# Linear attention on one core: v in whole rows, a touch of sixteen pieces, and a tenth warm-up matmul

## The chip, the cores and the metric

The kernel runs on one core of a Trainium2 chip. Its time is the device time of that core in microseconds (us), and the time of a kernel is the median of its runs. The engines named below are TensorE (PE for its matmuls, PEld for its weight loads), VectorE (DVE), ScalarE (ACT), GpSimd (POOL) and SyncE (SP), which here only issues transfers. Sixteen DMA engines move the data.

## What is computed

Inputs q, k and v have the shape (1, 32, 2048, 128) in bf16: 32 heads of 2048 rows by 128 columns. Each head is computed alone.

```python
phi_q = jnp.where(q > 0, q + 1, jnp.exp(q)) + 1e-6
phi_k = jnp.where(k > 0, k + 1, jnp.exp(k)) + 1e-6
kv = jnp.einsum("bhsd,bhse->bhde", phi_k, v)
z = jnp.einsum("bhsd->bhd", phi_k)
num = jnp.einsum("bhqd,bhde->bhqe", phi_q, kv)
den = jnp.einsum("bhqd,bhd->bhq", phi_q, z)[..., None] + 1e-6
return num / den
```

## The kernel before

Every engine gets a list of operations, each with a key; a small planner (`Plan`) sorts each engine's list by key and puts in the semaphore waits that the reads and writes ask for. TensorE's part of heads 1 to 30 is a hardware loop of five turns of six heads.

A head is cut into 16 tiles of 128 rows: partition p holds rows 16p to 16p+15, so that one partition's share of a head is 4 KB that lie together in memory. The feature map is split in two parts that are never added in full: `emk` = min(exp(k), 1) + 1e-6 and `rk` = max(k, 0), and the same for q with `emq` and `rq`. Per head the steps are these.

- SP issues the loads of k, q and v (line 386, 512 KB each) into six buffers each, `h % 6`. The first in its queue are k0, q0, v0, k1, q1, v1.
- ACT: `ek` = exp(k) (line 393). DVE: `emk` from it (line 399). POOL: `rk` (line 396; head 1 on DVE), and for tiles 1 to 5 (`ADD`) the sum of both parts (line 404).
- TensorE transposes the 16 tiles of q into `xT_ps` (line 432, "tr(h)"). ACT makes `eq` = exp of that (line 443; in head 0 in two halves), ACT and DVE make `rq` (lines 450, 452), DVE `emq` (line 464).
- TensorE multiplies phi_k by v into `kvz_ps` (line 414, "kv(h)"), for the 11 tiles of `SPLIT` once with `emk` and once with `rk`, for the five of `ADD` once with the sum. ACT copies the 128 columns to `kvs_sb` (line 423), DVE the z column (line 425, key "zs").
- TensorE multiplies phi_q by `kvs_sb` into `o_ps` ("num(h)", lines 480 and 481), and DVE divides (lines 502 to 524). SP stores the head (line 566).

In TensorE's list the order is tr(0), kv(0), tr(1), kv(1), num(0), tr(2), kv(2), num(1) and so on.

The sum z needs a column of ones beside v. In a v buffer, gaps of 32 columns that hold ones lie between groups of tiles: with GROUPS[buffer] = 1 there is a gap ahead of tile 0 and one behind tile 15; with 2 there is another between tiles 7 and 8. A tile at the edge of a group gets z from a matmul of 129 columns in place of 128, one gap column included. Every other tile needs one more matmul with the same weights, of a single column of ones (`mm_held`, line 344). With two groups v is loaded in half rows of 2 KB (lines 383 to 386). GROUPS is (1, 1, 1, 1, 2, 2), so heads with `h % 6` of 4 or 5 have half rows.

Ahead of the first head, TensorE runs nine matmuls of 500 columns on zeros ("warm-ups", lines 354 to 361; all but the first are at line 344). ACT's first instruction is a transfer of 64 bytes of v into a small tile of its own, `first_sb` (line 372, "the touch"); kv(0) has this transfer among the things it waits for.

Of the kernel before, what the change touches and what calls it, by code (L numbers as in the profile page):

```python
# [12 lines left out]
def _ap(base: bass.AP, elem_offset: int, dims):  # L13
    return bass.AP(base.tensor, base.offset + elem_offset, [list(base.ap[0])] + [list(d) for d in dims])
# [235 lines left out]
def bass_standalone__linear_attn_elu__prompt_kernel(  # L250
# [6 lines left out]
    B, H, S, D = q.shape  # L257
    assert D == P and S == 16 * P
    NT = 16
    NH = B * H  # L260
    bf16 = mybir.dt.bfloat16
    fp32 = mybir.dt.float32
    NBI = 6
# [7 lines left out]
    ADD = (1, 2, 3, 4, 5)  # L271
    SPLIT = tuple(j for j in range(NT) if j not in ADD)
    GAP = 32
    GROUPS = (1, 1, 1, 1, 2, 2)
    VW = NT * D + 3 * GAP

    qf = q.rearrange("b h s d -> (b h) s d")
    kf = k.rearrange("b h s d -> (b h) s d")
    vf = v.rearrange("b h s d -> (b h) s d")
    of = out.rearrange("b h s d -> (b h) s d")  # L280

    with ExitStack() as es:  # L282
        def sb(name, shape, dt):
            return es.enter_context(nc.sbuf_tensor(name, shape, dt))

        k_sb = sb("k_sb", [P, NBI, NT * D], bf16)
        v_sb = sb("v_sb", [P, NBI, VW], bf16)
        q_sb = sb("q_sb", [P, NBI, NT * D], bf16)
# [9 lines left out]
        o_sb = sb("o_sb", [P, NBO, NT, D], bf16)  # L298
        ident = sb("ident", [P, P], bf16)
        ones_sb = sb("ones_sb", [P, 1], bf16)  # L300
        first_sb = sb("first_sb", [1, 64], bf16)

        xT_ps = es.enter_context(nc.psum_tensor("xT_ps", [P, NT * P], bf16))
        kvz_ps = es.enter_context(nc.psum_tensor("kvz_ps", [P, 512], fp32))
# [14 lines left out]
        pl = Plan()  # L319
# [4 lines left out]
        vfull, ofull = v_sb[:, :, :], o_ps[:, :]  # L324
        xfull = xT_ps[:, :].bitcast(fp32)

        def vcol(bi, j):
            n = NT // GROUPS[bi]
            return GAP * (j // n + 1) + D * j, j % n == 0, j % n == n - 1
# [8 lines left out]
               reads=[("id0",)], writes=[("ident",)])  # L338
        n1 = GROUPS.count(1)
        pl.add("pool", -7, lambda g: g.memset(_ap(vfull, 0, [[VW, n1], [GAP + NT * D, 2], [1, GAP]]), 1.0), writes=[("vones", 1)])  # L340
        pl.add("pool", -6.5, lambda g: g.memset(_ap(vfull, n1 * VW, [[VW, NBI - n1], [GAP + NT * D // 2, 3], [1, GAP]]), 1.0),
               writes=[("vones", 2)])
        def mm_held(pe, out_ap, rhs, stop, start=False):
            return pe.add_instruction(mybir.InstMatmult(  # L344
                start_tensor_calc=start, stop_tensor_calc=stop, ldweights=False, bass_skip_group_check=True,
                tile_position=(0, 0), tile_size=(P, P), name=nc.get_next_instruction_name(), engine=mybir.EngineType.PE,
                ins=[pe.lower_ap(rhs), pe.lower_ap(held[0])], outs=[pe.lower_ap(out_ap)]))

        held = [None]
        WARM = 9  # L350

        def warm(pe):
            held[0] = zero_sb
            zeros = _ap(zero_sb, 0, [[0, 4], [1, 125]])
            for w in range(WARM):
                b = 2 + w % 3
# [12 lines left out]
                 ("zs", LAST): LAST - 1 + 0.902, ("kvs", LAST): LAST - 1 + 0.72}  # L369
        halves = {}  # L370

        pl.add("act", -20, lambda a: a.dma_start(first_sb[:, 32:64], vf[0, 0:1, 0:32]), writes=[("first",)], dma=("va", 0))

        for h in range(NH):
            def at(name, key, h=h):
                return place.get((name, h), h + key)
# [3 lines left out]
            def load(name, buf, src, key, h=h, bi=bi):  # L380
                dst, rws = buf[:, bi], rows(src, h)
                if name == "v":
                    n = GROUPS[bi]
                    dst = _ap(vfull, bi * VW + GAP, [[GAP + NT * D // n, n], [1, NT * D // n]])
                    rws = rws.rearrange("p (a b) -> p a b", a=n)
# [22 lines left out]
            def kv(pe, tiles, srcs, bi=bi, b3=b3):  # L408
                for j in tiles:
                    for src in srcs:  # L410
                        first, fin = (j == SPLIT[0] and src is emk_sb), j == ADD[-1]
                        w = src[:, b3, j * D:(j + 1) * D]
                        c, l, r = vcol(bi, j)
                        last = pe.matmul(kvz_ps[:, 1 - l:NC + r], lhsT=w, rhs=v_sb[:, bi, c - l:c + D + r], start=first, stop=fin,  # L414
                                         skip_group_check=True)
                        if not l + r:
                            held[0] = w
                            last = mm_held(pe, kvz_ps[:, 0:1], ones_sb[:, 0:1], fin)
                return last
            pl.add("pe", at("kv", -1.2), lambda pe, kv=kv: kv(pe, SPLIT, (emk_sb, rk_sb)),  # L420
                   reads=[("emk", b3), ("rk", b3), ("v", bi), ("ones",), ("vones", GROUPS[bi])] + ([("first",)] if h == 0 else []), writes=[("bankkv",)])
            pl.add("pe", at("kv", -1.2), lambda pe, kv=kv: kv(pe, ADD, (rk_sb,)), reads=[("phik", b3), ("v", bi)], writes=[("bankkv",)])
# [183 lines left out]
```

## Time and profile before

| | |
|---|---|
| median of 3 runs | 169.97 us (169.88 to 170.01) |
| the profiled execution | 169.75 us |
| its span in the profile | 168.0 us |
| PE busy | 159.1 us, 95% of the span |
| PEld / DVE / ACT / POOL busy | 91% / 90% / 93% / 62% |
| DMA queue 1 (all loads and stores) | 67.12 MB in 19856 packets, 99.0% of 16 engines |
| DMA queue 10 (the touch) | 2 packets |
| mean rate over the span | 400 GB/s |

Busy shares are averages over the start, the steady state and the end. A matmul's recorded duration is its latency, 217 ns for 128 columns, while matmuls that follow one another start 56 ns apart; so the pace is read from starts. "Idle before" names what ended the wait that came just ahead of an instruction.

### The profile page before, as it was taken

Reading aid. Unit: us, or ns where it says so; the run is one execution under the profiler, and the core shown is the slowest. Engines: PE = TensorE matmul, PEld = TensorE weight load, DVE = VectorE, ACT = ScalarE, POOL = GpSimd, SP = SyncE. Lnnn points to the kernel's source line nnn. Section 1 sums busy time; section 2 is a strip of 40 time slices with the busy share of each in tenths; the row PEclk is TensorE's granted clock in tenths of the full one; section 3 lists DMA queues with packets and bytes.
Section 4 is the critical chain, followed back from the end, with each engine's and each line's share of the span. In section 5 each row is a group of like instructions: output and inputs, shape, how many; then the busy total and the mean of one; then the engine's idle time right before and its main releaser. Section 6 shows DMA issues by size and latency. Waiting matters only on the chain.

```text
span 168.0 us, 6551 instructions
## 1 busy us (share of the span) xinstructions
PE 159.1 (95%) x3169; PEld 153.3 (91%) x2465; DVE 151.9 (90%) x298; ACT 155.6 (93%) x143; POOL 103.5 (62%) x71
## 2 busy tenths in 40 slices
PE   7689999999999999999999999999999999999960
PEld 0479999999999999999999999999999999999950
DVE  0367999999999999999999999999999999999971
ACT  3879999999999999999999999999999999997790
POOL 2717677666666777666667766666677766666300
PEclk9999999999999999999999999999999999999995
DMA  5999999999999999999999999999999999999955
GB/s 201 355 419 417 418 407 420 414 411 416 419 415 420 421 415 419 419 418 417 419 418 419 419 415 419 418 417 419 419 419 419 419 418 418 419 419 416 414 244 197
DMA packets 19869, 67.25 MB, mean 400 GB/s; under 512 B 2066, under 2 KB 2194, under 8 KB 19858
## 3 DMA queue, kind: packets, MB, share of 16 engines
q1 hardware_dynamic: 19856, 67.12, 99.0%
q8 instruction: 5, 0.08, 0.2%
q14 instruction: 6, 0.05, 0.1%
q10 hardware_dynamic: 2, 0.00, 0.0%
HBM read 50.33 MB, written 16.78 MB: 400 GB/s over the span
## 4 chain that ended last, share of the span: by engine, by line
PE 89%; DMA 4%; DVE 2%; ACT 1%; SPq 1%; issue 0%; DVEq 0%
PE kvz_ps L414 37%; PE o_ps L480 18%; PE o_ps L481 17%; PE xT_ps L432 16%; DMA k_sb<-in_k_dram 4%; DVE o_sb L520 1%; PE kvz_ps L344 1%; ACT ek_sb L393 1%; SPq L386 1%; DVE emk_sb L399 0%; DVE rden_sb L508 0%; DVE den_sb L502 0%; DVE o_sb L513 0%; DVEq L282 0%; DVE kvs_sb L425 0%
## 5 line engine op out<-in xcount | busy, mean ns | idle before, releaser
L404 POOL TENSOR_TENSOR rk_sb<-rk_sb,emk_sb 128x640 bf16<-128x640 bf16 x32 | 44.7, 1396 | 50.2 <-DVE emq_sb L464 44.5
L414 PE MATMUL kvz_ps<-v_sb,rk_sb 128*128 128x128 bf16 (+1 forms) x512 | 69.1, 217 | 0.0
L520 DVE TENSOR_TENSOR o_sb<-o_ps,rden_sb 128x768 bf16<-128x768 f32 (+2 forms) x62 | 67.8, 1134 | 0.0
L393 ACT ACTIVATE ek_sb<-k_sb 128x2048 bf16<-128x2048 bf16 x32 | 61.5, 1920 | 2.5 <-DMA k_sb<-in_k_dram 2.4
L443 ACT ACTIVATE eq_sb<-xT_ps 128x2048 bf16<-128x2048 bf16 (+1 forms) x33 | 60.1, 1825 | 3.7 <-PE xT_ps L432 2.5
L480 PE MATMUL o_ps<-kvs_sb,emq_sb 128*128 128x129 bf16 (+1 forms) x536 | 61.1, 217 | 0.2 <-DVE o_sb L513 0.2
L481 PE MATMUL o_ps<-kvs_sb,rq_sb 128*128 128x129 bf16 (+1 forms) x536 | 61.1, 217 | 0.0
L396 POOL TENSOR_SCALAR rk_sb<-k_sb 128x2048 bf16<-128x2048 bf16 x31 | 58.7, 1893 | 2.3 <-DMA k_sb<-in_k_dram 2.3
L344 PE MATMUL kvz_ps<-ones_sb,rk_sb 128*128 128x1 bf16 x428 | 59.6, 165 | 0.0
L414 PE MATMUL kvz_ps<-v_sb,emk_sb 128*128 128x128 bf16 (+1 forms) x352 | 56.8, 218 | 1.6 <-DMA v_sb<-in_v_dram 1.1
L480 PEld LDWEIGHTS o_ps<-kvs_sb,emq_sb 128*128 128x128 bf16 x536 | 50.6, 98 | 0.5 <-DVE o_sb L513 0.4
L481 PEld LDWEIGHTS o_ps<-kvs_sb,rq_sb 128*128 128x128 bf16 x536 | 50.1, 97 | 0.0
L414 PEld LDWEIGHTS kvz_ps<-v_sb,rk_sb 128*128 128x128 bf16 x512 | 46.7, 96 | 1.1
L344 PE MATMUL kvz_ps<-ones_sb,emk_sb 128*128 128x1 bf16 x268 | 44.0, 165 | 0.0
L414 PEld LDWEIGHTS kvz_ps<-v_sb,emk_sb 128*128 128x128 bf16 x352 | 33.8, 96 | 1.9 <-issue 1.2
L432 PE MATMUL xT_ps<-ident,q_sb 128*128 128x128 bf16 x512 | 34.5, 222 | 0.4 <-DMA q_sb<-in_q_dram 0.4
L432 PEld LDWEIGHTS xT_ps<-ident,q_sb 128*128 128x128 bf16 x512 | 30.6, 99 | 4.4 <-DMA q_sb<-in_q_dram 4.4
L450 ACT ACTIVATE rq_sb<-xT_ps 128x1024 bf16<-128x1024 bf16 x30 | 30.6, 1019 | 0.0
L399 DVE TENSOR_SCALAR emk_sb<-ek_sb 128x2048 bf16<-128x2048 bf16 x32 | 21.9, 684 | 6.0 <-ACT ek_sb L393 6.0
L452 DVE TENSOR_SCALAR rq_sb<-xT_ps 128x1024 bf16<-128x1024 bf16 x34 | 23.4, 691 | 2.8 <-ACT eq_sb L443 2.4
L464 DVE TENSOR_SCALAR emq_sb<-eq_sb 128x2048 bf16<-128x2048 bf16 x32 | 22.4, 699 | 0.0
L513 DVE TENSOR_TENSOR o_sb<-o_ps,rden_sb 128x128 bf16<-128x128 f32 x31 | 9.0, 291 | 1.1
(28 smaller groups left out, 47.6 us busy)
## 6 DMA issues: line engine op xcount, KB each, us to landing
k_sb<-in_k_dram SPq DMA_DIRECT2D x32, 512.0 KB, 14.3
q_sb<-in_q_dram SPq DMA_DIRECT2D x32, 512.0 KB, 14.1
v_sb<-in_v_dram SPq DMA_DIRECT2D x32, 512.0 KB, 14.3
out_dram<-o_sb SPq DMA_DIRECT2D x31, 512.0 KB, 14.9
out_dram<-o_sb SPq DMA_DIRECT2D x1, 288.0 KB, 3.3
out_dram<-o_sb SPq DMA_DIRECT2D x1, 224.0 KB, 3.2
first_sb<-in_v_dram ACTq DMA_DIRECT2D x1, 0.1 KB
```

What stands on the lines that cost most here:

```text
L344: return pe.add_instruction(mybir.InstMatmult(start_tensor_calc=start, stop_tensor_calc=stop, ldweights=False, bass_skip_group_check=True, ...
L393: lambda a, bi=bi, b2=b2: a.activation(ek_sb[:, b2, :], k_sb[:, bi, :], ACT.Exp),
L396: lambda e, bi=bi, b3=b3: e.tensor_scalar(rk_sb[:, b3, :], k_sb[:, bi, :], BIG, 0.0, op0=ALU.min, op1=ALU.max),
L404: pl.add("pool", h + 0.5, lambda g, added=added: g.tensor_tensor(out=added(rk_sb), in0=added(rk_sb), in1=added(emk_sb), op=ALU.add), reads ...
L414: last = pe.matmul(kvz_ps[:, 1 - l:NC + r], lhsT=w, rhs=v_sb[:, bi, c - l:c + D + r], start=first, stop=fin, skip_group_check=True)
L432: last = pe.transpose(xT_ps[:, j * P:(j + 1) * P], q_sb[:, bi, j * P:(j + 1) * P], ident[:])
L443: halves[part] = pl.add("act", key, lambda a: a.activation(eq_sb[:, b2, c], xT_ps[:, c], ACT.Exp), reads=both[part:part + 1] or both, writ ...
L450: f = lambda a: a.activation(rq_sb[:, b3, c], xT_ps[:, c], ACT.Relu)
L452: f = lambda d: d.tensor_scalar(rq_sb[:, b3, c], xT_ps[:, c], 0.0, None, op0=ALU.max)
L480: pe.matmul(o_ap, lhsT=emq_sb[:, b3, t * P:(t + 1) * P], rhs=kvs_sb[:, b3, c0:c1], start=True, stop=False)
L481: return pe.matmul(o_ap, lhsT=rq_sb[:, b3, t * P:(t + 1) * P], rhs=kvs_sb[:, b3, c0:c1], start=False, stop=True)
L520: pl.add("dve", key, lambda d: d.tensor_tensor(out=o_sb[:, bo, 3 * g0:3 * g1, :].rearrange("p (a b) d -> p a b d", b=3), in0=_ap(full, bas ...
```

## The change

All six v buffers have one group, so every v is loaded in whole rows of 4 KB, and the gaps of ones are two in each buffer. One POOL memset fills them; the second memset is gone. The touch reads 32 columns from each of 16 places of head 0's v, 32 KB apart, into 16 partitions. The warm-up has ten matmuls.

```diff
-    GROUPS = (1, 1, 1, 1, 2, 2)
-    VW = NT * D + 3 * GAP
+    GROUPS = (1, 1, 1, 1, 1, 1)
+    VW = NT * D + 2 * GAP
...
-        first_sb = sb("first_sb", [1, 64], bf16)
+        first_sb = sb("first_sb", [16, 64], bf16)
...
         pl.add("pool", -7, lambda g: g.memset(_ap(vfull, 0, [[VW, n1], [GAP + NT * D, 2], [1, GAP]]), 1.0), writes=[("vones", 1)])
-        pl.add("pool", -6.5, lambda g: g.memset(_ap(vfull, n1 * VW, [[VW, NBI - n1], [GAP + NT * D // 2, 3], [1, GAP]]), 1.0),
-               writes=[("vones", 2)])
...
-        WARM = 9
+        WARM = 10
...
-        pl.add("act", -20, lambda a: a.dma_start(first_sb[:, 32:64], vf[0, 0:1, 0:32]), writes=[("first",)], dma=("va", 0))
+        pl.add("act", -20, lambda a: a.dma_start(first_sb[:, 32:64], vf[0].rearrange("(p j) d -> p (j d)", p=NT)[:, 0:32]), writes=[("first",)], dma=("va", 0))
```

The order of the instructions on every engine stays as it was, apart from the memset that is gone, the added warm-up and four more single-column matmuls in each head of buffers 4 and 5.

## The prediction

> **What bounds the kernel now.** The chain of waits comes first: 89% of the span is TensorE work.
>
> ```profile
> PE 89%; DMA 4%; DVE 2%; ACT 1%; SPq 1%; issue 0%; DVEq 0%
> ```
>
> The list of waits from 12.1 to 160 us comes next. TensorE (PE, and PEld for its weight loads) waits only once there, for 0.5 us at 12.0 us; it never waits for a transfer.
>
> ```profile
> POOL rk_sb L404 <- DVE emq_sb L464: 44.5, 29, 1.8
> ...
> PEld kvz_ps L414 <- DVE kvs_sb L425: 0.7, 1, 0.7
> PE kvz_ps L414 <- DVE kvs_sb L425: 0.5, 1, 0.5
> ```
>
> So two things set the end: when kv(1), the KV product of head 1, starts (12.03), and how much TensorE work follows. For the second I cut the steady state into heads, from one head's first transpose to the next, and asked for the instructions on kvz_ps alone. Each row holds the stretch, its length, then busy time and count on PE, PEld, DVE and ACT. Head 8's transposes start at 44.91, and the rows below are heads 8 to 12.
>
> ```profile
> 44.91:49.75 4.84, 2.25 (x50) 2.12 (x27) 0.22 (x1) 0.29 (x1) 1.00 1.04 418
> 49.75:54.57 4.82, 2.25 (x50) 2.12 (x27) 0.22 (x1) 0.29 (x1) 1.00 1.04 419
> 54.57:59.30 4.73, 2.15 (x46) 2.01 (x27) 0.22 (x1) 0.29 (x1) 1.00 1.02 418
> 59.30:64.04 4.74, 2.15 (x46) 2.01 (x27) 0.21 (x1) 0.29 (x1) 1.00 1.02 416
> 64.04:68.86 4.82, 2.25 (x50) 2.12 (x27) 0.22 (x1) 0.29 (x1) 1.00 1.03 419
> ```
>
> The third and fourth rows are heads 10 and 11, whose v lies in buffers 4 and 5, in half rows: four matmuls fewer on kvz_ps, 0.10 us less PE time on it, and a head that is 0.08 to 0.11 us shorter. TensorE is busy through all of every stretch, so it is the bound in both kinds of head.
>
> For the start I read the timeline from 0 to 16 us (start, duration, engine, instruction, idle time before it in brackets).
>
> ```profile
> 4.12 1.91 ACT L393 ACTIVATE ek_sb<-k_sb 128x2048 bf16<-128x2048 bf16 x1 [1.56 <-DMA k_sb<-in_k_dram]
> 5.33 1.75 PE L432 MATMUL xT_ps<-ident,q_sb 128*128 128x128 bf16 x16 [0.38 <-DMA q_sb<-in_q_dram]
> 6.41 1.94 ACT L443 ACTIVATE eq_sb<-xT_ps 128x1024 bf16<-128x1024 bf16 x2 [0.38 <-PE xT_ps L432]
> 8.19 0.22 PE L414 MATMUL kvz_ps<-v_sb,emk_sb 128*128 128x129 bf16 x1 [1.10 <-DMA v_sb<-in_v_dram]
> 9.20 1.91 ACT L393 ACTIVATE ek_sb<-k_sb 128x2048 bf16<-128x2048 bf16 x1 [0.85 <-DMA k_sb<-in_k_dram]
> 11.14 0.69 DVE L399 TENSOR_SCALAR emk_sb<-ek_sb 128x2048 bf16<-128x2048 bf16 x1 [0.87 <-ACT ek_sb L393]
> 11.75 0.22 DVE L425 TENSOR_SCALAR kvs_sb<-kvz_ps 128x1 bf16<-128x1 f32 x1
> ```
>
> Head 1's k lands, ACT's exp of it runs from 9.20, DVE makes emk(1) from 11.14, then the z column of head 0, and only then kv(1) starts at 12.03. ACT stood idle 0.85 us before 9.20, after eq(0) ended at 8.35.
>
> Why is k late? The transfers are queued k0, q0, v0, k1, q1. Their times to landing, each asked for alone, are 3.4, 4.1, 6.3, 7.1 and 7.8 us; with the issue times 0.73, 1.18, 1.65, 2.11 and 2.59 they land at about 4.1, 5.3, 7.95, 9.2 and 10.4. All steps are 1.2 us but one: v0 comes 2.65 us behind q0, 1.4 too many, and all behind it are late by as much. In the trace's completion marks of the sixteen DMA engines, twelve had finished v0 by 6.77 and four came at 7.32, 7.45, 7.91 and 7.94. The DMA view of 5 to 8 us beside that of 8 to 11 says the same.
>
> ```profile
> DMA packets 281, 1.04 MB, mean 345 GB/s; under 512 B 28, under 2 KB 28, under 8 KB 281
> ...
> DMA packets 340, 1.25 MB, mean 418 GB/s; under 512 B 34, under 2 KB 34, under 8 KB 340
> ```
>
> The engines were busy 99% or more in both: packets took longer, nothing was missing in the queue.
>
> **Part 1, whole rows.** Ten of the 32 heads use buffers 4 and 5 (4, 5, 10, 11, 16, 17, 22, 23, 28, 29). In each, tiles 7 and 8 stop being edges: four 129-column matmuls become 128 wide, and four 128x1 matmuls are added, 50 in place of 46. From the starts of the transposes, 17 whole-row heads from 6 to 30 take 4.826 us on average and the eight half-row ones 4.735: +0.091 each. By single starts, a 128-column matmul with its 128x1 companion takes 0.082 and one alone 0.056, so 4 x 0.026 = +0.105 less four columns. I take the head period, since it holds everything: 10 x 0.091 = **+0.91 us**, bounds 0.85 and 1.05. Nothing covers it, as TensorE never waits there; ACT and DVE, busy 4.74 and 4.73 of head 9's 4.82 us, stay below. The DMA side, ten transfers in 128 pieces fewer each, shortens a queue for which TensorE doesn't wait, so 0; and it has an idle stretch of its own at 162 to 163 us (53 GB/s) ahead of the last stores. The POOL memset that goes (0.26 us at 1.65) and the one that grows lie inside POOL's 2.27 us of waiting for k0: 0.
>
> **Part 2, the touch.** Before, it moves one piece (queue 10 has 2 packets: data and semaphore), so one DMA engine meets v ahead of time. Now sixteen rows go out on the same ACT instruction, 32 KB apart over v0. The Trainium skill (DMA: Bandwidth & Descriptors, "Why a DMA increments its semaphore by 16 and not by 1") has a transfer of sixteen rows run on sixteen engines, one of a single row on one; the 2 packets here agree for the single row.
>
> If v0's 1.4 us is the price of an engine's first access to v, it goes away, and k1 lands at 8.0 to 8.2 (9.2 less the 1.2 that the last engine lost against the twelfth; twelve engines finished k1 by 8.22). Then ACT's exp of k1 starts when eq(0) ends, 8.35: a gain of at most **0.85**. Everything later moves along: q1, v1 and k2 (10.4, 11.7, 12.9) were late by the same amount; kv(1) at 11.18 would otherwise wait for v1.
>
> Against it, the touches now stand ahead of k0 on all engines (ACT issues at 0.73, as does SP). Their cost shows only in nearby rows: from 1.7 to 2.5 us k0's own first 36 packets took 89.7% of 16 engines x 0.8 us, 0.32 us each, against 0.161 from 3 to 4 us (101 data packets, 101.5% of 16 us), so a cold start costs an engine some 35 packets x 0.161 / 16 = 0.35 us. Bounds for the delay d of k0 and q0: 0 (the cold accesses overlap) and 1.4 (v0's whole stall falls on k0). q0 late by d moves tr(0), eq(0) and the exp of k1 alike, so the gain is 0.85 - d: +0.85 to -0.55. I take d = 0.4, the row of the same kind, so **-0.45 us**; no cure at all gives 0.
>
> **Part 3, the tenth matmul.** The warm-ups start 0.415 apart, the ninth at 4.33; a tenth starts at 4.75 and frees the array for tr(0) at 5.16. q0 lands at 5.3, or later by d. It fills the 0.38 us of idle: 0.
>
> **Sum.** The profiled execution took 169.75 (span 168.0 and 1.75 around it), 0.22 below the median of 169.97. 169.75 + 0.91 - 0.45 = 170.21, and against the median **170.4**.
>
> **The rivals.**
>
> Full cure without delay: d near 0, gain 0.85, 169.97 + 0.91 - 0.85 = 170.0, no change. For it: the one touch landed at 1.92 by its completion mark, 0.67 us after its issue ended (0.73 to 1.25), without delaying k0 by more than a last engine at 4.10 where fifteen had finished by 3.97. Against: k0's own cold start.
>
> No cure: v0's long packets are not about first access. For it: q0 was never touched and arrives a plain 1.2 us behind k0; and the longest packets in v0's time (0.67 to 1.05 us in the trace's packet records) start at 5.1 to 5.3, not with its first ones at 4.7. 169.97 + 0.91 = 170.9.
>
> The touch harms: k0 takes over the stall of 1.4 us: 169.97 + 0.91 + 0.55 = 171.4. Nothing but the serial length of v0's stall speaks for it.
>
> Faster, by the clock: tr(0) runs at 0.107 us a transpose until 6.8 us, though the granted clock reads 1.00; tr(1) at 0.056. If unbroken warm-ups bring full pace before 5.3, the first eight transposes are 0.41 us shorter, eq(0) starts when ek(0) ends (6.03), the exp of k1 at 7.97 if k1 is there: gain 1.23, 169.65. It decides only with the stall cured and d under 0.1. Against: nine warm-ups, 3.9 us of them, did not bring it. The Trainium skill (TensorE: Matmul & The Clock Gate, "What's actually happening") lets full pace come after one busy window of about 3.4 us in a free-running grid. By that rule the switch at 6.8 closes a window from 3.4, and a tenth matmul would change nothing unless the grid lies elsewhere in the next run; no view shows the grid.
>
> **How the numbers follow.** Part 1 paid and about half won back: 0.38, at 170.4 (own range 170.2 to 170.7). Full cure 0.22 at 170.0; no cure 0.20 at 170.9; harm 0.08 at 171.4; the clock 0.12 at 169.65. The range, 169.65 to 171.0, leaves out harm and the far side of the clock case, and holds the bounds of part 1. What a measurement can tell from no change is 0.2%, 0.34 us. Faster by more: most of the clock case, 0.10. Within: the full cure, the rest of that case and the near end of the forecast, 0.30. Slower: 0.60.
>
> **What would show it.** Part 1: 50 matmuls on kvz_ps in every head and all heads at 4.82 to 4.84; a head 10 still at 4.74 would prove it wrong. Part 2: 32 packets on queue 10; v0 about 1.2 us behind q0; k0 at 4.4 to 4.6 and ACT's idle time before the exp of k1 gone; kv(1) at about 11.6. v0 still 2.6 us behind q0 means no cure. Part 3: no idle before tr(0) or only d's. Wrong altogether: TensorE waiting after 13 us.

## The result, and the profile after

The changed kernel takes 170.99 us (median of 11 runs, 170.49 to 172.3), the kernel before 170.01 us (11 runs, 169.64 to 170.93): a ratio of 1.0067, interval 1.0052 to 1.0083, or +0.98 us by the medians, where +0.43 was forecast. The profiled execution took 171.06 us, span 169.1.

The chain of waits of the changed kernel still gives TensorE 89%.

```profile
PE 89%; DMA 4%; DVE 2%; ACT 1%; issue 1%; SPq 1%; DVEq 0%
```

The stretches of heads 8 to 12, the instructions on kvz_ps alone (stretch, length, busy time and count on PE, PEld, DVE, ACT, then clock, DMA share, GB/s):

```profile
45.24:50.08 4.84, 2.25 (x50) 2.12 (x27) 0.22 (x1) 0.29 (x1) 1.00 1.03 416
50.08:54.90 4.82, 2.25 (x50) 2.12 (x27) 0.21 (x1) 0.29 (x1) 1.00 1.02 414
54.90:59.72 4.82, 2.25 (x50) 2.12 (x27) 0.22 (x1) 0.28 (x1) 1.00 1.03 418
59.72:64.56 4.84, 2.25 (x50) 2.12 (x27) 0.22 (x1) 0.29 (x1) 1.00 1.02 415
```

Heads 10 and 11 (the last two rows) have 50 matmuls and take 4.82 and 4.84 where they took 4.73 and 4.74. So part 1 did to TensorE what was written.

The timeline of the start, and TensorE's first wait after it:

```profile
4.17 1.91 ACT L391 ACTIVATE ek_sb<-k_sb 128x2048 bf16<-128x2048 bf16 x1 [1.71 <-DMA k_sb<-in_k_dram]
5.49 1.07 PE L430 MATMUL xT_ps<-ident,q_sb 128*128 128x128 bf16 x16 [0.51 <-DMA q_sb<-in_q_dram]
7.11 0.22 PE L412 MATMUL kvz_ps<-v_sb,emk_sb 128*128 128x129 bf16 x1 [0.55 <-DMA v_sb<-in_v_dram]
...
10.98 0.23 PE L412 MATMUL kvz_ps<-v_sb,emk_sb 128*128 128x129 bf16 x1 [0.47 <-DVE kvs_sb L423]
...
17.16 0.22 PE L412 MATMUL kvz_ps<-v_sb,emk_sb 128*128 128x129 bf16 x1 [1.18 <-issue]
```

k0 is not delayed (exp of k0 at 4.17, before 4.12). tr(0) runs its sixteen transposes in 1.07 us (before 1.75). kv(0) starts at 7.11 (8.19), kv(1) at 10.98 (12.03): 1.05 us won, more than the forecast's 0.45. But kv(2) starts at 17.16 (16.87) after 1.18 us of idle time. "issue" means that the view found no releaser; the trace's completion marks have one: fifteen of the sixteen DMA engines had finished v2 by 15.80, the last at 17.07. All that was won is lost there, and 0.29 more.

What held the last engine is in the table of DMA queues of the changed kernel:

```profile
q1 hardware_dynamic: 18576, 67.12, 98.2%
q8 instruction: 5, 0.08, 0.2%
...
q10 hardware_dynamic: 32, 0.00, 0.0%
```

Queue 8 brings instructions in packets of 16 KB. In the trace's packet records one starts at 14.89 and takes 1.10 us, and two data packets that start right behind it, at 15.98 and 16.41, took 0.44 and 0.35 us where 0.16 is usual. The records don't name the engine; that all three are on the one that finished v2 last is read from these times. Before, that packet came at 15.65, and v2 was down at 16.72.

TensorE's last matmul ends at 163.67, 1.29 us later than before (162.38): 0.29 from the start and 0.98 from the ten heads, which are 0.097 to 0.099 us longer each. That looks like the whole loss, but it is not. These are the DMA views of 160 to 170 us, first before, then after. The first line is the rate in slices of 0.25 us from 160; the second is the issue of the last store but one: size and time to landing.

```profile
GB/s 442 361 328 246 246 213 180 115 82 49 66 16 213 393 410 410 410 295 339 365 385 381 391 248 28 26 29 22 0 0 0 0 0 0 0 0 0 0 0 0
...
out_dram<-o_sb SPq DMA_DIRECT2D x1, 288.0 KB, 3.3
```

```profile
GB/s 197 393 377 410 393 442 246 164 164 66 66 33 66 16 33 16 33 115 410 393 410 442 344 309 376 411 369 370 284 28 24 29 14 0 0 0 0 0 0 0
...
out_dram<-o_sb SPq DMA_DIRECT2D x1, 288.0 KB, 3.2
```

In both kernels the rate falls from about 400 to 22 to 29 GB/s for the last microsecond: one sixteenth, one DMA engine alone. The completion marks of the last store say the same: before, fifteen engines at 166.23 to 166.39 and the sixteenth at 167.49; after, 167.48 to 167.66 and 168.66. So two things race at the end. Fifteen engines follow TensorE: last matmul plus 4.0 us in both kernels. The sixteenth is a late engine (the marks name no engine; that it is one and the same is inferred from the rate of one sixteenth): by the last mark of each store it is behind the median engine by 1.8 us at 89 us of the changed kernel and by 4.5 at 159 (before 1.3 and 3.1), and it has never caught up when the stores end. It sets the time in both profiles. TensorE's end had 1.1 us of cover before the change and has 1.0 after it, so its 1.29 us are hidden save about 0.2 (167.66 against the old 167.49). The loss is that the late engine's own end went from 167.49 to 168.66.

### The profile page after: what moved, and what is told of

The parts are those of the page before. It is cut to its first block, busy times and chain, and to the rows that moved or that the text cites. A ratio compares the mean times of both kernels' runs of the same rounds, so it can differ in the third digit from the quotient of the medians.

```text
span 169.1 us, 6591 instructions
## 1 busy us (share of the span) xinstructions
PE 159.6 (94%) x3210; PEld 153.8 (91%) x2465; DVE 152.3 (90%) x298; ACT 156.1 (92%) x143; POOL 103.5 (61%) x70
## 4 chain that ended last, share of the span: by engine, by line
PE 89%; DMA 4%; DVE 2%; ACT 1%; issue 1%; SPq 1%; DVEq 0%
PE kvz_ps L412 37%; PE o_ps L478 17%; PE o_ps L479 17%; PE xT_ps L430 16%; DMA k_sb<-in_k_dram 4%; PE kvz_ps L342 1%; DVE o_sb L518 1%; ACT ek_sb L391 1%; SPq L384 1%; DVE emk_sb L397 0%; DVE rden_sb L506 0%; DVE den_sb L500 0%; DVE o_sb L511 0%; DVEq L282 0%; DVE kvs_sb L423 0%
## 5 line engine op out<-in xcount | busy, mean ns | idle before, releaser
L412 PE MATMUL kvz_ps<-v_sb,rk_sb 128*128 128x128 bf16 (+1 forms) x512 | 70.1, 217 | 0.0
L342 PE MATMUL kvz_ps<-ones_sb,rk_sb 128*128 128x1 bf16 x448 | 62.9, 165 | 0.0
L412 PE MATMUL kvz_ps<-v_sb,emk_sb 128*128 128x128 bf16 (+1 forms) x352 | 57.8, 218 | 2.2 <-issue 1.2
L342 PE MATMUL kvz_ps<-ones_sb,emk_sb 128*128 128x1 bf16 x288 | 47.2, 165 | 0.0
L430 PE MATMUL xT_ps<-ident,q_sb 128*128 128x128 bf16 x512 | 33.8, 219 | 0.6 <-DMA q_sb<-in_q_dram 0.5
L430 PEld LDWEIGHTS xT_ps<-ident,q_sb 128*128 128x128 bf16 x512 | 29.9, 98 | 4.6 <-DMA q_sb<-in_q_dram 4.6
```

Of the source, the lines that this page charges most:

```text
L342: return pe.add_instruction(mybir.InstMatmult(start_tensor_calc=start, stop_tensor_calc=stop, ldweights=False, bass_skip_group_check=True, ...
L430: last = pe.transpose(xT_ps[:, j * P:(j + 1) * P], q_sb[:, bi, j * P:(j + 1) * P], ident[:])
```

## The experiments

Each ratio is against runs of the kernel before that were made alongside. "Fifteenth" and "sixteenth" are the last two completion marks of the last store in that run's profile. A kernel without an interval was run once.

**e1, whole rows alone** (touch and warm-up as before).

```diff
-    GROUPS = (1, 1, 1, 1, 2, 2)
-    VW = NT * D + 3 * GAP
+    GROUPS = (1, 1, 1, 1, 1, 1)
+    VW = NT * D + 2 * GAP
...
-        pl.add("pool", -6.5, lambda g: g.memset(_ap(vfull, n1 * VW, [[VW, NBI - n1], [GAP + NT * D // 2, 3], [1, GAP]]), 1.0),
-               writes=[("vones", 2)])
```

> Only the whole rows, with one touch piece and nine warm-ups. Theory (the whole rows are paid for in full by TensorE, 10 heads x 0.095 us): start as before (kv(1) at 12.0, kv(2) at 17.0), every head 4.82 to 4.84 us, 170.95. Rival (the whole-row loads relieve the DMA and the sum of the change is a loss of something else): under 170.5.

170.96 us, 1.0070 (1.0052 to 1.0089): the whole loss is in this part.

**e2, the sixteen pieces alone.**

```diff
-        first_sb = sb("first_sb", [1, 64], bf16)
+        first_sb = sb("first_sb", [16, 64], bf16)
...
-... vf[0, 0:1, 0:32]) ...
+... vf[0].rearrange("(p j) d -> p (j d)", p=NT)[:, 0:32]) ...
```

> Only the touch of sixteen pieces; half rows in buffers 4 and 5 and nine warm-ups as before. Theory (the start gains 1 us, and kv(2) then waits for the last DMA engine's part of v2, which one 16 KB instruction transfer holds up): v0 lands 1.2 to 1.3 us behind q0, kv(1) at 11.0, kv(2) not before 17.0, 170.0 (169.8 to 170.2). Rival (the start's gain is kept and the loss comes from the whole rows alone): kv(2) at about 16.0, 169.0.

169.83 us, 0.9994 (0.9977 to 1.0011). The timeline of its start:

```profile
5.35 1.07 PE L432 MATMUL xT_ps<-ident,q_sb 128*128 128x128 bf16 x16 [0.84 <-DMA q_sb<-in_q_dram]
7.33 0.22 PE L414 MATMUL kvz_ps<-v_sb,emk_sb 128*128 128x129 bf16 x1 [0.91 <-DMA v_sb<-in_v_dram]
11.20 0.23 PE L414 MATMUL kvz_ps<-v_sb,emk_sb 128*128 128x129 bf16 x1 [0.49 <-DVE kvs_sb L425]
...
16.96 0.22 PE L414 MATMUL kvz_ps<-v_sb,emk_sb 128*128 128x129 bf16 x1 [0.76 <-issue]
```

kv(1) is 0.83 us early, kv(2) 0.09 late: v2's last engine finished at 16.87, behind an instruction packet of 1.06 us. The start's gain is real and ends at head 2. TensorE ended at 162.48 and the sixteenth mark stands at 167.63, as before.

**e3, the tenth warm-up alone** (`WARM = 10`).

> Only the tenth warm-up. Theory (it fills idle time and the moment at which full pace begins is not its doing): no idle of more than 0.2 us ahead of tr(0), v0 2.6 us behind q0 as before, 170.0 within 0.2. Rival (unbroken warm-ups bring full pace before tr(0)): all sixteen transposes of tr(0) 0.056 us apart in this profile, and a time 0.2 to 0.4 us shorter only if k1 is there by then, which it is not (9.2).

169.94 us, 1.0009 (0.9996 to 1.0023). By accident it tests the end too: in its profile TensorE ended 0.95 us later than before (163.33), and the fifteenth mark came at 167.35, the sixteenth at 167.79. That execution took 170.05, 0.30 more than before: two thirds of TensorE's delay were covered.

**e4, both start edits, with v2 issued ahead of k3** (half rows).

```diff
-            load("v", v_sb, vf, h - NBI - 0.8)
+            load("v", v_sb, vf, h - NBI - (0.87 if h == 2 else 0.8))
```

> Sixteen pieces and ten warm-ups, half rows as before, and SP issues v2 ahead of k3 in place of behind it. Theory (kv(2) waits for v2's data): v2 lands by 14.6, TensorE does not wait at kv(2) (about 15.9); the wait moves to k3, for which ACT's exp of head 3 now waits until 15.8, or 17.1 if the instruction transfer again holds up one engine, and eq(2) behind it: time between 169.0 and 170.5. Rival (TensorE waits at kv(2) for its own instructions, whose transfer runs at that time): kv(2) still starts at about 17.1 with v2 landed 2.5 us earlier.

170.03 us, 1.0018 (0.9996 to 1.0039). The timeline of TensorE and of ACT:

```profile
15.72 0.22 PE L414 MATMUL kvz_ps<-v_sb,emk_sb 128*128 128x129 bf16 x1
...
17.18 1.91 ACT L393 ACTIVATE ek_sb<-k_sb 128x2048 bf16<-128x2048 bf16 x1 [2.92 <-DMA k_sb<-in_k_dram]
```

With v2 early, kv(2) doesn't wait. So the 1.18 us that the view gives to "issue" were a wait for v2, not for TensorE's own instructions. But k3 takes v2's place behind the instruction packet (last engine at 17.16): ACT's exp of it waits 2.92 us, and tr(3) starts at 21.71, 0.9 later than before. The wait moves with the last transfer in the queue.

**e5, TensorE's work of the changed kernel on the loads and layout of the kernel before.** The edges of the middle gap are no longer used.

```diff
-            return GAP * (j // n + 1) + D * j, j % n == 0, j % n == n - 1
+            return GAP * (j // n + 1) + D * j, j == 0, j == NT - 1
```

> Loads and SBUF layout as before (half rows in buffers 4 and 5), but TensorE works as in the changed kernel: tiles 7 and 8 are no edges, so 50 matmuls on kvz_ps in every head. Theory A (TensorE's work sets the end): heads of 4.83 us throughout and 170.95, the same loss as with the whole rows. Theory B (the end is set by one late DMA engine, which in the profile of before finishes the last store at 167.5 where the other fifteen finish by 166.4, so TensorE has 1.1 us of slack, and the whole rows make that engine later): 170.0 to 170.2.

170.09 us, 1.0032 (1.0008 to 1.0057): +0.20 us by the medians, 0.54 by the ratio, whose interval reaches 0.97 us. The times alone therefore don't exclude that the whole 0.91 is paid; the marks, and e9 and e10 below, do that. All heads take 4.82 to 4.84, and TensorE ends at 163.77, 1.38 later than before. The marks stand at 167.77 and 167.87: TensorE's end has just caught up with the late engine.

**e6, whole rows without the added matmuls.** e1 less the single-column matmuls of tiles 7 and 8 in buffers 4 and 5; z of the ten heads lacks these two tiles.

```diff
-                        if not l + r:
+                        if not l + r and not (bi > 3 and j in (7, 8)):
```

> Whole rows in all buffers, one touch piece and nine warm-ups, but the single-column matmuls of tiles 7 and 8 are left out in the heads of buffers 4 and 5, so z lacks these tiles there and TensorE has as much work as before. Theory A: 170.0. Theory B: 170.9, with heads of 4.73 us in buffers 4 and 5 and one DMA engine late by over 2 us against the fifteen others at the last store.

171.03 us, 1.0058 (1.0035 to 1.0081), with heads 10 and 11 back at 46 matmuls:

```profile
56.30:61.02 4.72, 2.15 (x46) 2.01 (x27) 0.22 (x1) 0.28 (x1) 1.00 1.03 420
61.02:65.76 4.74, 2.15 (x46) 2.01 (x27) 0.22 (x1) 0.29 (x1) 1.00 1.03 417
```

The loss stays without the work that was to cause it. The sixteenth mark stands at 168.83, 0.56 behind the fifteenth and not the "over 2 us" that was expected. So the harm comes through the transfers.

**e7 and e8, the sixteen pieces taken elsewhere**: from q of head 0 (e7), from v of the last head (e8), in place of v of head 0; half rows, nine warm-ups.

```diff
-... vf[0].rearrange("(p j) d -> p (j d)", p=NT)[:, 0:32]) ...
+... qf[0].rearrange("(p j) d -> p (j d)", p=NT)[:, 0:32]) ...
```

> As e2, but the sixteen pieces are read from head 0's q in place of its v. Theory (v0's delay is the price of an engine's first access to v): v0 lands 2.3 to 2.8 us behind q0 as before, kv(0) after 8.0. Rival (sixteen small transfers ahead of k0 help whatever they read, by setting the engines out of step): v0 1.2 to 1.5 us behind q0.

> As e2, but the sixteen pieces are read from the last head's v, 16 MB behind v0. If what an engine meets first is the whole region of v: v0 1.2 to 1.8 us behind q0 as in e2. If it is the neighbourhood of the addresses touched: 2.3 to 2.8 us as before.

170.0 and 169.85 us, one run each. v0 lands 1.39 us behind q0 in e7 (6.78) and 1.25 in e8 (7.08), where it was 2.65 behind. The stall goes although nothing touches head 0's v, so it isn't the price of a first access to v0. One profile each would be thin, but the others agree: in all eleven profiles with one touch piece v0 lands 2.2 to 2.9 us behind q0, and in five of the six with sixteen pieces, whatever they read, 1.2 to 1.8.

**e9 and e10, the tiles kept where they were.** e9 is e1, and e10 the changed kernel, each with the old width of v_sb; the third gap is unused. Nothing else differs.

```diff
-    VW = NT * D + 2 * GAP
+    VW = NT * D + 3 * GAP
```

> As e1 (whole rows, one touch piece, nine warm-ups), but VW keeps its third gap of 32 columns, unused, so every v buffer and every tile behind v_sb stays at its old SBUF address. Theory L (the whole-row kernels lose because the new SBUF addresses slow the DMA packets, which took 159 ns in the kernels with the old addresses and 160 to 172 in the others from 11 us on): packets at 159 ns again, 170.0 to 170.2. Theory H (the half rows kept the DMA engines from colliding): 170.9 and packets above 159 ns as in e1.

> The changed kernel whole, with the third gap kept in VW and nothing else altered. Theory L: its loss goes away, 169.8 to 170.2, although TensorE has all the added matmuls. Theory H: 171.0.

e9: 169.90 us, 1.0023 (0.9997 to 1.0049). e10: 169.87 us, 1.0008 (0.9994 to 1.0021). All of the changed kernel's work is in e10, and its loss is gone. The unused columns are never read or written; all they do is to keep the v buffers 64 bytes further apart, and q_sb and the tiles behind it 384 bytes a partition higher. In the DMA view of the end of e10 no engine is left alone (366, 58, 0):

```profile
GB/s 147 115 82 295 410 393 410 377 311 49 49 16 33 16 33 16 33 0 0 0 377 393 442 410 410 232 369 396 378 366 366 58 0 0 0 0 0 0 0 0
...
out_dram<-o_sb SPq DMA_DIRECT2D x1, 288.0 KB, 2.2
```

In this execution (170.52 us) TensorE was the later of the two, with marks at 168.24 and 168.26. Its start shows that the touch is no sure cure either:

```profile
8.29 0.22 PE L412 MATMUL kvz_ps<-v_sb,emk_sb 128*128 128x129 bf16 x1 [1.78 <-DMA v_sb<-in_v_dram]
```

With the same sixteen pieces, v0 came at 8.04, 2.65 behind q0. e9's profile (171.79) is an outlier of another kind, told at the end.

**e11, half rows and TensorE's work as before, on the changed kernel's addresses.** v_sb gets the smaller width; buffers 4 and 5 share gaps with their neighbours so that three gaps still fit; the memset, the loads and the matmuls take `vat(bi)` for `bi * VW`.

```diff
-    VW = NT * D + 3 * GAP
+    VW = NT * D + 2 * GAP
...
+        def vat(bi):
+            return bi * VW - (GAP if bi > 3 else 0)
```

> Half rows in buffers 4 and 5, one touch piece, nine warm-ups as before, TensorE's work as before, but v_sb as long as in the changed kernel: buffers 0 to 3 at the changed kernel's addresses, 4 and 5 sharing gaps with their neighbours, all tiles behind v_sb at the changed kernel's addresses. Theory L: 170.8 to 171.1 and packets above 159 ns from 11 to 14 us on. Theory H: 170.0.

171.32 us, 1.0096 (1.0080 to 1.0112). The DMA view of its end:

```profile
GB/s 393 442 393 426 344 279 246 180 197 164 82 66 66 33 360 377 442 393 393 271 401 360 409 360 410 116 56 45 47 18 28 28 22 29 7 0 0 0 0 0
...
out_dram<-o_sb SPq DMA_DIRECT2D x1, 288.0 KB, 4.4
```

TensorE ends at 162.79, and yet the last store drags on for some two microseconds with one to four engines, 4.4 us from issue to landing. The addresses alone make the loss.

**e12, e1 with 384 unused bytes a partition behind v_sb**, so that q_sb and the rest are at their old places and v_sb keeps its new width.

```diff
         v_sb = sb("v_sb", [P, NBI, VW], bf16)
+        pad_sb = sb("pad_sb", [P, NBI * GAP], bf16)
         q_sb = sb("q_sb", [P, NBI, NT * D], bf16)
```

> As e1, with v at the changed kernel's addresses (stride 2112), but an unused tile of 384 bytes behind v_sb, so that q_sb and all later tiles are at their old addresses. Under theory L this tells which address it is: 171.0 if it is the stride of the v buffers, 170.0 to 170.2 if it is the place of q_sb, o_sb or another tile behind.

170.27 us, 1.0039 (1.0007 to 1.0071), lowest 169.87. Three kernels at the new addresses (e1, e6, e11) never ran below 170.8 us. The sixteenth mark is level with the fifteenth, 168.02 and 168.01. So it isn't the spacing of the v buffers, which is the changed kernel's here.

**e13, e14 and e15: which tile, and is it the place or the alignment?** e13 puts e12's pad behind q_sb, so that only q_sb stands lower. e14 is e12 with 128 more bytes in front of o_sb, which puts the stores' tile where the changed kernel has it modulo 512. e15 is the kernel before with 128 unused bytes in front of q_sb:

```diff
         v_sb = sb("v_sb", [P, NBI, VW], bf16)
+        pad_sb = sb("pad_sb", [P, 2 * GAP], bf16)
         q_sb = sb("q_sb", [P, NBI, NT * D], bf16)
```

> Whole rows alone (e1) with an unused tile of 384 bytes a partition behind q_sb: q_sb stands where the changed kernel has it, o_sb and all tiles between where the kernel before has them. If it is q_sb's place that lengthens the transfers' packets: the share of 4 KB packets at 159 ns falls below 60% by 14 to 24 us, as in e1 (97, 70, 72, 42, 24% by windows of 2 us from 12 us), and the time is e1's, 170.8 to 171.2 us. If it is o_sb's place: over 90% at 159 ns, and e12's time, 169.9 to 170.4.

> Whole rows alone with 384 unused bytes behind v_sb (e12: q_sb at its old place) and 128 more in front of o_sb, so that o_sb stands 128 bytes higher than before, which modulo 512 is where the changed kernel has it. If q_sb's place decides, or if o_sb's place matters only by itself and not modulo 512: e12's 169.9 to 170.4 with over 80% of packets at 159 ns. If o_sb's place modulo 512 decides: 170.8 to 171.2 and packets as in e1.

> The kernel before with 128 unused bytes a partition between v_sb and q_sb: half rows, work and order all as before, q_sb at 50432 bytes behind k_sb's start plus nothing else, which is 256 modulo 512 as in the changed kernel (before: 128). If the place of q_sb modulo 512 (or 256) decides: packets disturbed and 170.8 to 171.4 us, 0.5 to 0.9% over before, as e11 (1.0096). If only the absolute place or another tile's place counts: 169.9 and 98% of packets at 159 ns.

e13: 171.28 us, 1.0074 (1.0060 to 1.0088). e14: 170.29, 1.0029 (1.0012 to 1.0046). e15: 170.85, 1.0058 (1.0045 to 1.0072). So it is q_sb's place and not o_sb's, and it needs no other edit: the kernel before, with 128 unused bytes, loses 1.06 us by the medians. (In e15 the tiles behind q_sb move by 128 bytes too; e13 moves q_sb alone.) By the ratios alone e12 and e13 would not be told apart, since their intervals overlap; the lowest times, 169.87 and 170.91, and the packets and marks below tell them apart. e13's end, for comparison with e10's:

```profile
GB/s 246 164 295 426 377 459 360 361 180 147 98 66 82 33 16 16 33 33 16 377 377 410 393 442 233 413 383 375 384 365 92 24 22 22 0 0 0 0 0 0
...
out_dram<-o_sb SPq DMA_DIRECT2D x1, 288.0 KB, 3.1
```

All of them together. The share is that of the 4 KB packets in the trace's records from 14 to 24 us that took 159 ns or less; the start of q_sb is in bytes a partition from the start of k_sb, added up from the sizes of the tiles in the kernel.

| kernel | q_sb at | modulo 256 | share at 159 ns | fifteenth | sixteenth | ratio |
|---|---|---|---|---|---|---|
| before | 50304 | 128 | 100% | 166.39 | 167.49 | 1 |
| e2 touch | 50304 | 128 | 99% | 166.48 | 167.63 | 0.9994 |
| e5 PE work | 50304 | 128 | 100% | 167.77 | 167.87 | 1.0032 |
| e9 rows, old width | 50304 | 128 | 100% | 169.33 | 169.34 | 1.0023 |
| e10 change, old width | 50304 | 128 | 99% | 168.24 | 168.26 | 1.0008 |
| e12 rows, pad | 50304 | 128 | 93% | 168.01 | 168.02 | 1.0039 |
| e14 rows, two pads | 50304 | 128 | 99% | 167.24 | 167.59 | 1.0029 |
| after | 49920 | 0 | 38% | 167.66 | 168.66 | 1.0067 |
| e1 rows | 49920 | 0 | 48% | 169.28 | 169.30 | 1.0070 |
| e6 rows, cut | 49920 | 0 | 45% | 168.27 | 168.83 | 1.0058 |
| e11 half rows | 49920 | 0 | 41% | 167.52 | 169.05 | 1.0096 |
| e13 q_sb alone | 49920 | 0 | 48% | 168.02 | 168.94 | 1.0074 |
| e15 before + 128 | 50432 | 0 | 73% | 167.93 | 168.81 | 1.0058 |

Where the sixteenth mark stands clear of the fifteenth, it lies at 167.5 to 167.9 with the old place and at 168.7 to 169.1 with the others. e3, e4, e7 and e8, all at the old place, have shares of 99 to 100% and sixteenth marks of 167.59 to 167.81. Where the two are level, TensorE was late in that execution and the late engine is hidden. An earlier mark isn't hidden: the last mark of head 25's store is at 159.40 to 159.95 in all eleven profiles with q_sb at the old place, and at 160.87 to 161.38 in all six with another. Why e12 and e14 are 0.5 us over the kernel before and e9 and e10 hardly at all is open; the intervals of e9, e12 and e14 overlap. No kernel tried is clearly faster than the one before: e2, e9 and e10 are level with it, since a gain needs both TensorE's end and the late engine's to come earlier.

## Why the prediction was wrong

**What bounds the kernel.** "So two things set the end: when kv(1) ... starts, and how much TensorE work follows" is the step that failed first. Both were read rightly, but the end is set by the later of two, TensorE plus 4.0 us and the late engine, and before the change the late engine was 1.1 us behind. The chain of waits hides this: its PE share is the same 89% when a store's last engine is the last thing to end. The page of before gave a sign: 3.3 us for a store of 288 KB, against 2.2 in e10, where nothing lags.

**Part 1, TensorE.** The term, +0.91, is about right as work: ten heads by 0.098 us, 0.98 in sum. "Nothing covers it, as TensorE never waits there" is wrong. It cost +0.20 by the medians of e5 and vanished in e9 (1.0023, at most 1.0049 or 0.83 us) and in e10 (1.0008, at most 1.0021 or 0.36 us), which have all of it. An engine without idle time can still have cover, behind its last instruction.

**Part 1, the transfers.** "The DMA side ... so 0" is where the loss lay: +1.17 us on the late engine in the profiles, shown by e6 (without TensorE's part) and e11 (without whole rows as well). It isn't the count of packets, which the prediction weighed; it is the `VW` line of the diff, which the prediction read as a matter of gaps. It moves q_sb by 384 bytes, and packets take longer. Mean durations of 4 KB packets, before and after: 159.3 and 160.9 ns from 40 to 80 us, 159.4 and 160.1 from 80 to 120, 159.2 and 159.6 from 120 to 150, and about 3 ns apart from 12 to 36. An estimate for one engine, which starts a packet every 0.159 us: 150 x 3 + 250 x 1.6 + 250 x 0.7 + 190 x 0.4 = 1.1 us. The size fits, but the marks don't bear the estimate out for every engine: at head 25's store the median engine is 0.02 us later than before (156.64 and 156.63), and the last one 1.19 (160.87 and 159.68). Nor is the mean of 12 to 36 us a sure sign, as e2 has 163.3 ns there, as much as the changed kernel (163.0), and loses nothing. So the place of q_sb is shown to make the loss; how it falls on one engine is open. That the forecast of part 1 came near the measured loss is accident.

**Part 2, the touch.** The size at kv(1) was off. d is 0.04 us for k0 (4.14 by its marks, before 4.10) and 0.16 for q0 (5.45, before 5.29) in place of 0.4. And tr(0) ran at full pace, so that eq(0) ended at 8.09 in place of 8.35 though q0 came later, and the exp of k1 began at 8.15 in place of 9.20. The gain was 1.05 in place of 0.45, over the bound of 0.85, which took tr(0) at its old pace. The step that failed is "Everything later moves along": v2 does not, and kv(2) takes the gain back (e2: 0.9994). The condition, "the price of an engine's first access to v", fell with e7, and e10 shows that v0 can be late with the sixteen pieces in place. Why v0 stalls stays open.

**Part 3, the tenth matmul.** 0 was right (e3). The prediction's faster rival asked for full pace in tr(0); it came in the changed kernel, but also in e2 with nine warm-ups (1.07 us for sixteen transposes), so the tenth isn't its cause. The prediction took the clock of the start to be 1.00 and wrote that "no view shows the grid". The trace's clock records say when full clock begins. In the kernel before, the first record of full clock starts at 6.79 us, just where the transposes go from 0.107 to 0.056 us; ahead of it there is no record, and the views print 1.00. In the changed kernel that record starts at 4.45 and in e2 at 3.92, ahead of tr(0), and over all seventeen profiles at 3.73 to 6.79, with nine warm-ups and with ten. So the moment differs from one execution to the next.

**The signs.** 50 matmuls in every head, 32 packets on queue 10 and v0 about 1.4 us behind q0 (1.2 was written) all came, and ACT's idle time before the exp of k1 was gone. k0 at 4.4 to 4.6 and kv(1) at about 11.6 did not come: 4.14 and 10.98. "Wrong altogether: TensorE waiting after 13 us" came too, at 17.16; it was the right alarm for part 2, but no sign was set for the end of the stores, where the time went.

## What to carry to other kernels

Before a bound engine's added work is charged in full, look at what ends after its last instruction: if the rate of the last microsecond is that of one DMA engine, the end belongs to a late engine, and added work is free until it catches up. An edit that changes the size of a tile moves every tile behind it: build a control that keeps the old size as padding, since 128 bytes can cost more than the edit itself. A gain at the start counts only once every transfer of the next heads has been shown to come earlier too.

## What the runs showed of the hardware

**A load target's place in SBUF changes the time of its packets.** With q_sb at 50304 bytes from k_sb's start, 93 to 100% of the 4 KB packets from 14 to 24 us took 159 ns or less; at 49920 or 50432, 38 to 73%. The disturbance starts at 11 to 14 us, ahead of the first store's issue (21 to 22 us). The two bad places are multiples of 256, the good one isn't, and they lie on both sides of it, so an alignment is likely; with three places tried it isn't shown, and why a bad place for one of three load targets lengthens packets at large is open. The Trainium skill (DMA: Bandwidth & Descriptors, "How a descriptor splits into AXI transactions") has a read that starts off a multiple of 256 bytes cost extra beats. Here the better place is the one off it, though on the writing side of a load, and no run shows where k_sb itself starts.

**One of sixteen DMA engines is slower on stores.** By the steps of the marks, a store's share of 32 KB takes the last engine 1.38 us against 1.25 to 1.27 for the median engine, in the kernel before and after alike; loads take both about 1.25. After some thirty stores it was 3.1 us late at 159 us of the kernel before. The Trainium skill (DMA: Bandwidth & Descriptors, "Latency and other measured facts") has two engines that are usually slower than the others, and as a guess lays it to transfers whose descriptors are written by software. The trace agrees that an engine is slower, but for one alone, and it moves all loads and stores over a queue of the kind hardware_dynamic (q1), so that guess does not fit here; no run shows a cause.

**Instruction packets share the data's engines.** One of 16 KB kept an engine for 0.88 to 1.10 us and held back that engine's part of v2 or k3. The Trainium skill (Runtime: NRT & Kernel Launch, "Instruction fetch mechanics") calls the cost of such a fetch mostly hidden. For the fetching engine no run shows otherwise; for the transfer behind it, kv(2) waited 1.18 us in the changed kernel and e4 shows that the wait follows the transfer.

**The granted clock can fall at the start.** The clock changes at multiples of 3.41 us from its first record on. In nine of the seventeen profiles TensorE was busy for only 1.38 to 1.59 us of the first 3.41 us after the first record of full clock, and in all nine the clock of the next step is 0.50; in the other eight it was busy for 1.66 to 2.85 us, and the clock stays at 1.00. So, as far as these profiles go, about 1.8 us without work in such a step was enough, and 1.75 was not. This is e9's profile in three windows (length, PE busy time and count, granted clock, DMA share, GB/s):

```profile
4.00:8.00 4.00, 1.82 (x19) 0.98 0.99 353
8.00:12.00 4.00, 3.68 (x53) 0.50 1.03 411
12.00:16.00 4.00, 4.00 (x64) 0.67 1.02 419
```

After a wait of 2.07 us for v0 the clock is 0.50, and kv(0) and tr(1) run at half pace; e9's TensorE ended at 165.32. (e15 waited 1.39 us and its clock fell; e10 waited 1.78, across the end of a step, and its clock did not.) The profile of e15 has the same 0.50 from 8 to 12 us, yet its sixteenth mark stands 0.9 us clear of the fifteenth: there too the late engine set the time. e9's two executions with a mean clock of 0.975 took 171.79 and 172.03 us, the other ten 169.62 to 171.13.
